# One Trainium2 core: a linear-attention, gated-unit and mixer kernel whose weight conversion, channel layer and one normalisation are rearranged

## The chip, the cores and the metric

The kernel runs on one core of a Trainium2 chip. Five engines work side by side: TensorE (PE in the profile; PEld is its weight load), VectorE (DVE), ScalarE (ACT), GpSimd (POOL) and SyncE (SP), which here only issues transfers; GpSimd issues some too. The metric is the device time of one execution in microseconds (us); lower is better.

## The reference

Three layers follow one another, on 4 batches of 768 tokens with 384 features (8 heads of 48). Weights are given as float64, all else as float32.

```python
# 1. delta-rule attention, a state of 48x48 per batch and head
k_n = k / (norm(k) + 1e-6)
for t in range(S):
    y[:, :, t] = einsum('bhd,bhde->bhe', q[:, :, t], state)
    v_old = einsum('bhde,bhd->bhe', state, k_n[:, :, t])
    state = state + beta_t * einsum('bhd,bhe->bhde', k_n[:, :, t], v[:, :, t] - v_old)
# 2. gated unit: x is [4, 768, 384]
h = gelu_tanh(x @ w_in)                      # 1024 columns
u, v = h[..., :512], h[..., 512:]
v_n = (v - mean(v)) / sqrt(var(v) + 1e-6) * g_ln
v_s = einsum('ts,bsd->btd', w_sg, v_n) + b_sg[None, :, None]
x = x + (u * v_s) @ w_out
# 3. token mixing, then channel mixing
u = x + (relu(x^T @ w_tok1) @ w_tok2)^T      # 768 -> 256 -> 768
out = u + relu(u @ w_ch1) @ w_ch2            # 384 -> 1536 -> 384
```

## The kernel before

The attention is computed in chunks of 64 tokens, in six groups g (two pairs of batches, three stretches of 256 tokens). For each group TensorE forms Gram products (`kk`, `qk`: L134 and L159), VectorE solves a triangular system in 31 steps (`solve`, L179 to L221: two operations a step, L209 and L211), its result td is copied by transfers into tw (L230, issued by SyncE), TensorE makes three small products of it (`merge`: L242, L252, L264), and then the `chain` of 16 steps runs through four chunks (L305, L291, L281). The chain needs yr, a product made on GpSimd by `vput` (L273). `vput(g+1,0)`, for the next group's first chunk, is issued in the last step of chain g, the later ones inside the chain. The order of the work is written out by hand: one string for every chain step in the table `ACT` at the end of the file names what is issued there: K and Q Gram products, m a part of a merge, S a step of the solve, v a `vput`, l the loads of v (by GpSimd), z zeroing, c a step of `beside`.

`beside` is `conv` (L491 to L494): the float64 words of w_in are turned into a float32 pair, high and low part. `load` does it in 12 pieces of 256 columns: a load on SyncE (L456), five VectorE operations (L469 to L476), a copy on ScalarE for the high part (L444), a subtraction on GpSimd (L445), and two GpSimd transfers into a scratch in DRAM (L487). The steps 'c' stand in chains 0 to 2, what is left runs ahead of chain 3. Tiles for it come from a pool of their own, which `room()` closes after that to make space for xn of batches 2 and 3. `zeros` (L108, L112) is 12 ScalarE copies of zeros into tiles of the attention: four before anything else, the rest one for each step of the first solve from step 9 on.

Every dense product is made of three matmuls (high x high, high x low, low x high), `mm3`, L547 to L549. With chain 5 the dense part begins (`start`, `pre`): the scratch is loaded into SA as w_in (L699), `trans(0)` transposes batch 0 (L571, evacuated in L564), `V(0)` makes the V half (six pieces of 512 columns) and `U(0)` the U half (eight pieces of 384). One step of these is issued for each step of chain 5. Two PSUM banks serve them until `rest` adds six. `evV` evacuates a piece of V: square (ScalarE, L577), L578 and L581 on VectorE around a Tanh (ScalarE, L580), mean and variance (L586, L587), a power on GpSimd (L589), the normalise on VectorE (L591), and the split into a high copy (ScalarE, L444) and a low part (GpSimd, L445). Beside this the conversions of w_sg and w_out run. Then `Sg`, `V`, `Out`, `U` and `trans` follow for the batches, then the token mixing.

The channel layer (`chan`, L657 to L677) takes 8 half-batches of 384 tokens. For each of 12 f it makes 9 matmuls, w_ch1 stationary and the tokens moving, a Relu on ScalarE (L638) and the low part on VectorE (L639); one f later 9 matmuls with those results stationary and w_ch2 moving add to three accumulators of 384 columns. At the end xn takes three adds (L676) and three transfers out (L677). The 18 transposes of a batch stand between the batches. The weights w_ch1 and w_ch2 are converted beside the token mixing and the first half-batch.

## Time and profile before

| | |
|---|---|
| time, median of 3 runs | 981.63 us (979.33 to 985.21) |
| the profiled execution's own time | 980.1 us |
| its span | 978.4 us |
| TensorE busy | 856.8 us (88%), 9644 instructions |
| VectorE busy | 613.8 us (63%) |
| ScalarE busy | 391.2 us (40%) |
| GpSimd busy | 338.2 us (35%) |
| chain that ended last | TensorE 65%, VectorE 19%, ScalarE 4%, issue 4%, transfers 3%, GpSimd 2% |

Busy times are sums over one execution. The chain that ended last is followed back from the last instruction, at each step to what released it. The stages: up to 95 us the first Gram products and the first solve; 95 to 267 the solves, merges and chains 0 to 3; 267 to 298 chain 4; 298 to 351 chain 5 with V and U of batch 0; 351 to 548 the gated unit; 548 to 657 its end and the token mixing; 657 to 978 the channel layer, its first half-batch up to 701.6.

### The profile page before, as it was taken

The page shows a single profiled execution, that of the slowest core. Times are in us where ns is not written, and L with a number is a line of the kernel's source. Part 1 is how long each engine was busy: PE and PEld are TensorE (multiplying, and loading weights), DVE is VectorE, ACT ScalarE, POOL GpSimd, SP SyncE. Part 2 cuts the span into 40 slices and gives each one's busy share as a digit, 9 for nine tenths or more (in the row PEclk, how much of TensorE's full clock was granted, in tenths as well). Part 3 has the DMA queues.
Part 4 walks back from the last instruction along what each step waited for, and adds up shares of the span by engine and source line. Part 5 has one row for each costly group of instructions (what it writes and reads, how often), then busy time and mean ns, then how long its engine had stood idle before and what let it go on. Part 6 is the DMA issues. An engine that isn't in the chain of part 4 may idle for free.

```text
span 978.4 us, 23130 instructions
## 1 busy us (share of the span) xinstructions
PE 856.8 (88%) x9644; PEld 812.9 (83%) x9644; DVE 613.8 (63%) x1254; ACT 391.2 (40%) x869; POOL 338.2 (35%) x434
## 2 busy tenths in 40 slices
PE   6456764878788899999999998989899999999998
PEld 4346764867787689999999987879899999999998
DVE  5999998989902787947839896878513213123122
ACT  4525543758787663423423432434212112112111
POOL 7330475777763534323234443834200000000000
PEclk9679776979999999999999997999999999999999
DMA  6564748675444040000000022224100000000000
GB/s 160 148 144 107 174 122 193 170 169 138 122 95 147 1 163 31 1 1 1 1 1 0 30 69 65 87 87 127 50 1 25 25 1 25 1 25 25 1 25 25
DMA packets 60344, 68.05 MB, mean 70 GB/s; under 512 B 30416, under 2 KB 37328, under 8 KB 60240
## 3 DMA queue, kind: packets, MB, share of 16 engines
q1 hardware_dynamic: 58288, 59.49, 23.3%
q0 software_dynamic: 1952, 7.08, 2.3%
q8 instruction: 76, 1.25, 0.5%
q14 instruction: 28, 0.23, 0.1%
HBM read 51.61 MB, written 7.86 MB: 61 GB/s over the span
## 4 chain that ended last, share of the span: by engine, by line
PE 65%; DVE 19%; ACT 4%; issue 4%; DMA 3%; POOL 2%; SPq 1%; DVEq 0%; ACTq 0%; POOLq 0%
PE ps L547 18%; PE ps L548 18%; PE ps L549 18%; DVE p L209 4%; DVE T L211 3%; DVE F L471 2%; DVE F L472 2%; DMA tw<-td 2%; PE yp L281 2%; PE gm L134 1%; PE gm L264 1%; PE ps L571 1%; DVE F L473 1%; PE ck L305 1%; PE gm L252 1%
## 5 line engine op out<-in xcount | busy, mean ns | idle before, releaser
L639 DVE SCALAR_TENSOR_TENSOR hlo<-ps,hh 128x384 fp32r<-128x384 f32 x96 | 53.5, 557 | 206.2 <-ACT hh L638 206.2
L638 ACT ACTIVATE hh<-ps 128x384 fp32r<-128x384 f32 x96 | 47.2, 491 | 227.1 <-PE ps L549 227.1
L547 PE MATMUL ps<-GU,SB 128*128 128x384 f32 x288 | 97.6, 339 | 0.0
L549 PE MATMUL ps<-GU,SB 128*128 128x384 f32 x288 | 97.5, 339 | 0.0
L548 PE MATMUL ps<-GU,SB 128*128 128x384 f32 x288 | 97.2, 338 | 0.0
L209 DVE TENSOR_TENSOR p<-Li,T 128x87 f32<-128x87 f32 (+15 forms) x186 | 81.2, 449 | 3.8
L211 DVE TENSOR_TENSOR T<-T,p 128x87 f32<-128x87 f32 (+15 forms) x186 | 74.2, 412 | 3.8
L548 PE MATMUL ps<-SB,VHt 128*128 128x384 f32 x192 | 65.0, 338 | 2.3 <-POOL SB L445 2.3
L549 PE MATMUL ps<-VHt,hlo 128*128 128x384 f32 x192 | 65.3, 340 | 1.3 <-DVE hlo L639 1.3
L547 PE MATMUL ps<-SB,VHt 128*128 128x384 f32 x192 | 65.0, 338 | 0.0
L547 PE MATMUL ps<-VHt,hh 128*128 128x384 f32 x192 | 65.0, 338 | 0.0
L548 PE MATMUL ps<-VHt,hh 128*128 128x384 f32 x192 | 64.6, 337 | 0.0
L549 PE MATMUL ps<-SB,VHt 128*128 128x384 f32 x192 | 64.5, 336 | 0.0
L614 POOL TENSOR_TENSOR q<-q,u 128x384 f32<-128x384 f32 x32 | 36.9, 1158 | 66.1 <-DVE q L613 66.1
L305 PE MATMUL ck<-yr,tw 128*64 128x48 f32 x768 | 38.1, 239 | 23.0 <-POOL yr L273 12.7
L273 POOL TENSOR_TENSOR yr<-v,nn 64x192 f32<-64x192 f32 x96 | 54.3, 566 | 9.0 <-DMA v<-in_vn_dram 2.2
L145 POOL TENSOR_SCALAR_AFFINE_SELECT aq<-aq 32x512 f32<-32x512 f32 x48 | 38.0, 791 | 55.6 <-ACT aq L142 50.7
L305 PEld LDWEIGHTS ck<-yr,tw 128*64 128x64 f32 x768 | 32.8, 151 | 26.8 <-POOL yr L273 14.7
L547 PE MATMUL ps<-X,SA 128*128 128x384 f32 x144 | 49.9, 346 | 5.8 <-DVE xn L626 3.2
L548 PEld LDWEIGHTS ps<-GU,SB 128*128 128x128 f32 x288 | 54.1, 188 | 0.9 <-DVE GU L564 0.9
L547 PEld LDWEIGHTS ps<-GU,SB 128*128 128x128 f32 x288 | 54.1, 188 | 0.6 <-DVE GU L564 0.6
L549 PEld LDWEIGHTS ps<-GU,SB 128*128 128x128 f32 x288 | 54.0, 188 | 0.3 <-POOL SB L445 0.3
(155 smaller groups left out, 2357.3 us busy)
## 6 DMA issues: line engine op xcount, KB each, us to landing
kq<-in_kq_dram SPq DMA_DIRECT2D x48, 256.0 KB, 4.3
st<-in_ch_dram SPq DMA_DIRECT2D x36, 256.0 KB, 2.8
...
```

The costliest lines, as they stand in the source:

```text
L145: if blk==0: nc.gpsimd.affine_select(out=a,in_=a,pattern=[[0,8],[-64,2],[1,32]],compare_op=ALU.is_gt,fill=0.0,base=0,channel_multiplier=-1)
L209: nc.vector.tensor_tensor(p,Li[:,j,j+1:].unsqueeze(1).to_broadcast([128,w,n]),T[:,:w,j].unsqueeze(2).to_broadcast([128,w,n]),ALU.mult)
L211: nc.vector.tensor_tensor(T[:,:w,j+1:],T[:,:w,j+1:],p,ALU.add)
L273: n0=8*h+cc; nc.gpsimd.tensor_tensor(YRs[bb][gc%3][T_[par],:,par,:],VS[bb][T_[par],n0:n0+7:2,:],NNs[g%3][T_[par],16*bb+n0:16*bb+n0+7:2].un ...
L281: nc.tensor.matmul(yps[bb][o0:o0+64,2*pair+par,:],aq[F_,par,pair,cc,:],yr[F_,pair,par,:],start=True,stop=True)
L305: nc.tensor.matmul(u2[T_[par],pair,:],tw[F_,par,16*bb+8*h+2*pair+cc,:],yr[F_,pair,par,:],start=True,stop=True)
L547: nc.tensor.matmul(ps,L[0],Rr[0],start=first,stop=False)
L548: nc.tensor.matmul(ps,L[0],Rr[1],start=False,stop=False)
L549: nc.tensor.matmul(ps,L[1],Rr[0],start=False,stop=last)
L614: nc.gpsimd.tensor_tensor(gt,gt,u2[:,d,t],ALU.mult)
L638: nc.scalar.activation(hi,ps,AF.Relu)
L639: nc.vector.scalar_tensor_tensor(lo,ps,0.0,R(hi),op0=ALU.max,op1=ALU.subtract)
```

## The change

- w_in: only the columns of the V half (six pieces) are converted through the scratch, in steps 8 to 15 of chain 4, two steps of the generator at a time, ahead of `vput(5,0)`. The tiles are parts of attention tiles that are no longer used (`Spare`). The high copy moves from ScalarE to VectorE. The U half (six pieces) is loaded and converted straight into SA beside `trans(0)` and `V(0)`, a piece step for every second of theirs, and what is left ahead of `U(0)`.
- zeros: none ahead of the first products; one for each step of the first solve from step 1 on.
- all four xn are allocated at the start; `room` goes, and an unused branch on `qd`.
- V: the normalise is an Identity activation on ScalarE with scale rs and bias sf = -mean x rs, which a VectorE operation on one column makes.
- channel layer: six blocks of 512 tokens. The transposes of the next block (`tblk`) are issued within the present one from f = 6 on, into one of two buffers UB. In the second product w_ch2 is stationary and the 512 tokens move, so the output is transposed (OT); `out` adds the high and the low part of the block's input in two VectorE operations of 512 columns, and one transfer for each third of the features follows. The host's `unpack` turns the output back.

The diff, cut to what is spoken of:

```diff
-        for _ in range(4): next(zs)
@@ phase_a, first solve
-            if ns>8: next(zs,0)
+            if ns>0: next(zs,0)
@@ phase_a
+        class Spare:
+            def __init__(self):
+                v=lambda t,o,n:t.rearrange("p a b -> p (a b)")[:,o:o+n]
+                self.b=dict(st=[v(Lis[0],0,512),v(Lis[0],512,512),v(MD,0,512)],F=[v(MD,512,256),v(MD,768,256)],
+                    sq=[PP[0][:,0:256]],sh=[v(Ts[0],0,256),v(Ts[0],256,256)],sl=[v(Ts[0],512,256),v(Ts[0],768,256)])
...
-            if g==3 and beside is not None:
-                for _ in beside: pass
-                room()
+            if g==4 and beside is not None: bs=beside(Spare())
             if g==5 and tail is not None:
                 while wait: tick()
+                for _ in bs: pass
...
-                    if a=='c' and beside is not None: next(beside,0)
+                    if a=='c':
+                        for _ in range(n_): next(bs,0)
@@ load
-                    split(Fs[j],w[0],w[1],True)
+                    nc.vector.tensor_copy(w[0],Fs[j]); nc.gpsimd.tensor_tensor(w[1],Fs[j],R(w[0]),ALU.subtract)
@@ conv
-        yield from load(I['win'],None,None,[(0,3072,0)],pool=PX,lag=cfg.get('lag',1),g=cfg.get('cg',2),out=...)
+        yield from load(I['win'],None,None,[(1024*k+512,1024*k+1024,512*k) for k in range(3)],pool=PX,out=...)
@@ late2
-            L.UT=[a.rearrange("p (k t) -> p k t",t=768) for a in hl(GU,0,2304)]
+            L.UB=[[a.rearrange("p (k t) -> p k t",t=512) for a in hl(GU,3072*i,1536)] for i in range(2)]
@@ evV
+            sf=PT.tile([128,1],F32,name="sf")
             yield 1
-            nc.vector.tensor_scalar(v2,v2,mv[:,0:1],rs,ALU.subtract,ALU.mult)
+            nc.vector.scalar_tensor_tensor(sf,mv[:,0:1],-1.0,rs,op0=ALU.mult,op1=ALU.mult)
             yield 1
+            nc.scalar.activation(v2,v2,AF.Identity,bias=sf,scale=rs)
             split(v2,VH[0][:,s],VH[1][:,s],True)
@@ channel layer
+        def tblk(i):
+            for k in range(3):
+                ps=bank()
+                for j in range(4):
+                    b,n=divmod(4*i+j,6)
+                    nc.tensor.transpose(ps[:,128*j:128*j+128],xn[b][:,n,128*k:128*k+128],idt)
+                push(evT(ps,L.UB[i%2][0][:,k],L.UB[i%2][1][:,k]))
+                yield 1
-        def chan(b,hf,need):
-            acc=[psB[2].tile([128,512],F32,name="ps")[:,:384] for _ in range(3)]
+        def chan(i,need,nxt):
+            acc=[psB[2].tile([128,512],F32,name="ps") for _ in range(3)]
+            ut=L.UB[i%2]; hd=[None]*12
+            def out(e):
+                o=ph[0].tile([128,512],F32,name="o",bufs=2)
+                nc.vector.tensor_tensor(o,acc[e],R(ut[0][:,e]),ALU.add)
+                nc.vector.tensor_tensor(o,o,R(ut[1][:,e]),ALU.add)
+                nc.sync.dma_start(OT[:,e,512*i:512*i+512],o)
...
-                    for i in range(3):
-                        mm3(acc[i],[h[:,128*i:128*i+128] for h in hd[f-1]],[w[:,f-1,:] for w in C2A] if f<9 else [w[:,f-9,:] for w in L.C2B],f==1,f==12)
+                    for e in range(3):
+                        w=[w[:,f-1,128*e:128*e+128] for w in C2A] if f<9 else [w[:,f-9,128*e:128*e+128] for w in L.C2B]
+                        mm3(acc[e],w,hd[f-1],f==1,f==12)
+                        if f==12: out(e)
                     yield 1
+                if f>5: next(nxt,0)
@@ pre
-            for h in (1,0):
-                for i in range(2):
-                    nc.sync.dma_start(R(WIN[i])[:,:,512*h:512*h+512],scr[i].rearrange("p (k f) -> p k f",f=1024)[:,:,512*h:512*h+512])
-            yield from trans(0,XT)
-            yield from V(0)
+            for i in range(2): nc.sync.dma_start(R(WIN[i])[:,:,512:1024],scr[i].rearrange("p (k f) -> p k f",f=512))
+            ld=lw('win',WIN,[(1024*k,1024*k+512,1024*k) for k in range(3)])
+            yield from both(trans(0,XT),ld,cfg['u0'])
+            yield from both(V(0),ld,cfg['u1'])
+            for _ in ld: pass
             yield from U(0)
@@ rest
-                for b in range(4):
-                    go(both(chan(b,0,need),ld,n[2])); go(both(chan(b,1,need),ld))
-                    if b<3: go(trans(b+1,L.UT))
+                for i in range(6):
+                    go(both(chan(i,need,tblk(i+1) if i<5 else iter(())),ld,n[2]))
@@ tables
+for i in range(8,16): ACT[4][i]+=' c2'
```

## Rows read from the trace of the kernel before

**Rows 1.** stages: stretch, length, busy us (instructions) by engine, PE clock, DMA share, GB/s

```profile
95.00:267.00 172.00, 123.94 (x3586) 116.50 (x3587) 161.75 (x354) 102.97 (x244) 116.57 (x183) 0.83 0.65 156
267.00:298.00 31.00, 26.76 (x923) 25.20 (x923) 1.82 (x1) 25.62 (x61) 16.77 (x32) 1.00 0.41 89
298.00:351.00 53.00, 47.00 (x527) 39.26 (x523) 32.10 (x58) 35.33 (x81) 21.69 (x30) 0.97 0.36 127
351.00:548.00 197.00, 194.67 (x1081) 186.70 (x1080) 146.49 (x270) 79.09 (x166) 69.11 (x71) 1.00 0.03 9
...
657.00:701.60 44.60, 39.57 (x217) 37.68 (x217) 35.54 (x90) 18.48 (x51) 17.27 (x19) 1.00 0.27 83
701.60:978.40 276.80, 273.01 (x1568) 271.21 (x1566) 67.48 (x125) 48.52 (x102) 0.00 (x0) 1.00 0.05 18
```

**Rows 2.** waits from 95 to 299 us: us in total, times, longest

```profile
PE gm L242 <- DMA tw<-td: 17.9, 7, 7.1
...
DVE Li L183 <- DMA md<-gf: 2.2, 1, 2.2
```

**Rows 3.** SyncE's queue in time: start us, us; idle before in brackets

```profile
156.62 4.95 SPq L230 DMA_DIRECT2D tw<-td  x4
```

**Rows 4.** TensorE in time: chain 1's start, a merge, chain 5's start

```profile
128.82 1.68 PE L305 MATMUL ck<-yr,tw 128*64 128x48 f32 x18 [4.92 <-POOL yr L273]
...
162.40 0.29 PE L242 MATMUL gm<-tw,G 128*32 128x32 f32 x2 [7.14 <-DMA tw<-td]
166.65 1.07 PE L242 MATMUL gm<-tw,G 128*32 128x32 f32 x32 [3.96 <-DMA tw<-td]
...
298.26 1.11 PE L305 MATMUL ck<-yr,tw 128*64 128x48 f32 x31
```

**Rows 5.** VectorE by line, 95 to 267 us: busy us, mean ns; conversion, first and last

```profile
L469 DVE TENSOR_TENSOR sq<-st 128x256 f32<-128x256 f32 x12 | 6.3, 568 | 0.0
...
L471 DVE TENSOR_SCALAR F<-st 128x256 int32<-128x256 int32 x12 | 4.9, 447 | 0.0
```

**Rows 6.** GpSimd in time before chain 1

```profile
126.32 0.75 POOL L445 TENSOR_TENSOR sl<-F,sh 128x256 fp32r<-128x256 f32 x1
...
128.14 1.79 POOL L273 TENSOR_TENSOR yr<-v,nn 64x192 f32<-64x192 f32 x3
```

**Rows 7.** ScalarE in time at the start: zeros

```profile
7.01 3.99 ACT L108 COPY aq<-XZ 64x1024 f32<-64x1024 f32 x4 [4.94 <-DVE XZ L92]
```

**Rows 8.** GpSimd in time before chain 5

```profile
289.09 1.11 POOL L79 DMA_DIRECT2D v<-in_vn_dram  x2
...
292.42 2.25 POOL L273 TENSOR_TENSOR yr<-v,nn 64x192 f32<-64x192 f32 x4 [2.22 <-DMA v<-in_vn_dram]
```

**Rows 9.** VectorE in time, normalise of V(0) pieces

```profile
317.02 0.55 DVE L591 TENSOR_SCALAR q<-q,mv,rs 128x512 f32<-128x512 f32 x1 [0.16 <-POOL rs L589]
...
328.12 1.52 DVE L591 TENSOR_SCALAR q<-q,mv,rs 128x512 f32<-128x512 f32 x1
```

**Rows 10.** ScalarE by line, 400 to 548 us, shapes apart: high copy of V

```profile
L444 ACT CAST VHt<-q 128x512 fp32r<-128x512 f32 x15 | 9.3, 617 | 26.4 <-DVE q L591 26.4
```

**Rows 11.** waits from 298 to 351 us

```profile
PE ps L547 <- DVE q L581: 4.7, 5, 2.1
```

**Rows 12.** TensorE in time: V(0) pieces begin; 512-column matmuls

```profile
308.44 0.50 PE L547 MATMUL ps<-SA,X 128*128 128x512 f32 x1
...
311.67 0.50 PE L547 MATMUL ps<-SA,X 128*128 128x512 f32 x1
...
380.08 0.39 PE L547 MATMUL ps<-SA,X 128*128 128x512 f32 x1
...
382.12 0.39 PE L547 MATMUL ps<-SA,X 128*128 128x512 f32 x1
```

**Rows 13.** stage of one channel half-batch

```profile
701.65:739.60 37.95, 37.95 (x218) 37.92 (x218) 8.29 (x16) 5.91 (x12) 0.00 (x0) 1.00 0.05 16
```

**Rows 14.** VectorE in time at the end

```profile
973.60 1.60 DVE L676 TENSOR_TENSOR xn<-xn,ps 128x384 f32<-128x384 f32 x3 [1.00 <-PE ps L549]
```

More of the change, by code (lines that the diff above doesn't have):

```diff
@@ L28, in pack, with phase_a @@
     return dict(kq=half(tr(K)),qt=half(tr(Q)),vn=natv(V),kn=kn,bt=c(bt).reshape(2,3,128,32))
-def phase_a(tc,I,xn,cfg,tail=None,beside=None,room=None):
+def phase_a(tc,I,xn,cfg,tail=None,beside=None):
     nc=cfg.get('wrap',lambda x:x)(tc.nc)
@@ L389, in phase_a, with tile @@
         vput(0,0)
+        class Spare:
[3 more added lines that the diff above has]
+                    sq=[PP[0][:,0:256]],sh=[v(Ts[0],0,256),v(Ts[0],256,256)],sl=[v(Ts[0],512,256),v(Ts[0],768,256)])
+                self.n={}
+            def tile(self,shape,dt,name,bufs=1):
+                b=self.b[name]; assert len(b)>=bufs,(name,bufs)
+                i=self.n[name]=self.n.get(name,-1)+1
+                x=b[i%bufs].bitcast(dt) if dt!=F32 else b[i%bufs]
+                return x.rearrange("p (a b) -> p a b",b=2) if len(shape)==3 else x
         kt=[12]; mt=[8]
@@ L491, in load, with conv @@
             yield 1
-    def conv(PX,scr):
-        yield from load(I['win'],None,None,[(0,3072,0)],pool=PX,lag=cfg.get('lag',1),g=cfg.get('cg',2),out=lambda r:(scr[0][:,r],scr[1][:,r]))
+    def conv(scr,PX):
+        yield from load(I['win'],None,None,[(1024*k+512,1024*k+1024,512*k) for k in range(3)],pool=PX,out=lambda r:(scr[0][:,r],scr[1][:,r]))
     me.conv=conv
@@ L795 @@
 _m=dict(m=(0,1,9,10,11,12,13,14)); _k=dict(K=(1,2,5,6))
[L796 to L797 removed]
+ACT=[_row([3]*6+_st[6:],K=(3,4,6,7),Q=(9,10,12,13),m=range(9,15),l=(9,),v=(15,),q=(14,)),
+     _row(_st,z=(0,),**_k,**_m,**_s),_row(_st,z=(0,),**_k,**_m,**_s),_row(_st,z=(0,),**_m,**_s),
      _row([3]*9+[0]*7,z=(0,),m=(0,1,8,9,10,11,12,13,14,15),Q=(4,5,6,7),l=(9,),v=(15,)),_row([0]*16)]
[L799 removed]
+for i in range(8,16): ACT[4][i]+=' c2'
+CFG={'nl':(0.5,0.2,0.7),'k0':(1,3,5,7),'q0':(11,13,15,17),'l1':20,'late':2,'far':3,'tl':2,'half':21,'hs':5,'u0':0.5,'u1':0.5,'act':ACT}
 def build(tc,I,O,cfg):
     with tc.tile_pool(name="per",bufs=1,side="right") as pp, tc.tile_pool(name="scr",bufs=1,space=bass.MemoryType.DRAM) as pd, tc.manual_schedule():
[L803 removed]
+        xn=[pp.tile([128,6,384],F32,name=f"xn{b}") for b in range(4)]
         d=_dense(tc,I,O,xn,cfg)
[L805 to L814 removed]
+        scr=[pd.tile([128,1536],F32,name=f"scr{i}") for i in range(2)]
+        phase_a(tc,I,xn,cfg,lambda:d.start(scr),lambda P:d.conv(scr,P))
+        d.rest()
 def kernel(**inputs):
```

34 lines of the change are left out of this document (7 added, 27 removed).

## The prediction

> **What bounds the kernel now.** I read the table by stages first, since the shares of the whole span mix stages with different limits [rows 1]. It falls into three parts. From 351 us to the end TensorE is the bound: 194.67 us busy of 197, and 273.01 of 276.8 at a granted clock of 1.00. There only fewer or shorter matmuls help, or fewer stalls at the seams: the first channel half-batch takes 44.6 us, the next 37.95. Before 267 us nothing is full: between 95 and 267 TensorE is busy 123.94 us of 172, at a granted clock of 0.83, and VectorE 161.75. A busy share of 94% suggests that VectorE sets the pace, and the change takes work from it. The waits of that stretch say less [rows 2]: TensorE waits 17.9 us for the transfer of the solved matrices (tw<-td), and VectorE itself stands 2.2 us for its own input (md<-gf). The queues show what stands between: SyncE issues the four tw loads only from 156.62, after the loads ahead of it, and takes 4.95 us for them [rows 3], and TensorE's waits for that one set are 7.14 and 3.96 us, 11.1 of the 17.9 [rows 4]. So at least there VectorE was not last.
>
> From 298 to 351 (last chain, V and U of batch 0) TensorE is busy 47.0 of 53 us with VectorE and ScalarE at 32.1 and 35.3 [rows 1].
>
> **The change part by part.**
>
> *The conversion leaves chains 0 to 2.* Twelve pieces go, each five VectorE operations, from 568 to 447 ns on the average, five lines of 12, together 28.6 us [rows 5], a copy on ScalarE, a subtraction of 0.75 us and two DMA issues on GpSimd, and a load on SyncE. What of this is on the path?
> - GpSimd: at chain 1's start TensorE waits 4.92 us for yr [rows 4]. The products on GpSimd that make it began at 128.14, right behind a subtraction of the conversion that began at 126.32 [rows 6]; another such piece stands ahead of that, so two pieces, 1.82 us each (126.32 to 128.14), 3.64 us, are removed from just this wait. I take -3.6, bounds 0 (ScalarE's part is late next) and -4.9 (the wait vanishes).
> - VectorE: 28.6 us come off an engine that is 94% busy. TensorE can get back at most what it waits for the solves: 17.9 us. Of these the 11.1 us above are SyncE's and the DMA's. That leaves 6.8. VectorE, once faster, stands longer for md<-gf, whose chain through TensorE, ScalarE and SyncE is not shortened. I take -4, nearest to the 6.8; bounds 0 and -17.9.
> - SyncE: twelve loads less ahead of md and tw; -1, bounds 0 and -3 (an estimate: a load's issue is taken as a tw issue, 4.95/4 = 1.2 us, and two or three of them stand ahead of a late load).
> Together -8.6.
>
> *Zeros.* Four ScalarE copies of 1 us stand at 7.01 to 11.0, ahead of the first copies of Gram products [rows 7]. They are spread over the first solve, a step at a time, which ScalarE has time for. But TensorE's first products end only shortly before and the solve starts later through a DMA; -1.5, bounds -4.0 (all four) and +1 (a zero now stands ahead of a copy of a later group).
>
> *The V half in chain 4.* VectorE is idle there (1.82 us busy of 31 [rows 1]), so its 6 times 5 operations, and the copy that moves to it, cost nothing. The cover is that idle stretch, which ends with the last chain's transposes; without it they would cost about 17 us (half of 28.6 and six copies at about half a microsecond). GpSimd has no such room. Its queue runs v loads at 289.09 and then the products for chain 5 at 292.42, ready at 294.67 [rows 8]; TensorE starts chain 5 at 298.26 [rows 4]. The change puts six subtractions and twelve DMA issues ahead of those products: 6 x (0.75 + 2 x 0.555) = 11.2 us, behind the v loads' end at 290.2. The products then run 301.4 to 303.6, and chain 5 starts 5.3 us later. Behind the same queue stand the identity for the transposes, the two small scalings and the next products, so nothing of it comes back at once. Before, GpSimd waited for DMAs there, which will have landed; I take +5.0, bounds +2 (the subtractions start earlier than 290.2, as GpSimd's masks of the last group come earlier) and +7 (the loads of w_in from scratch late too).
>
> *U half beside trans(0) and V(0), normalise on ScalarE.* Per piece of V VectorE gives up the normalise, which took 0.55 us alone and 1.52 us beside a GpSimd subtraction [rows 9], and gets a tiny operation. It gets six pieces of four operations in place. ScalarE gets an Identity pass over 512 columns, priced like its 512-column copy at 617 ns [rows 10]. So per piece: VectorE has four passes of 512 columns, 3 x 0.55 + 1.52 = 3.2 us at the least, and comes to 1.7 plus about 2 us of conversion; ScalarE goes from three passes to four, 1.85 to 2.47 us, plus the chain's copies and a conversion's, an estimated 3.7, against 3.2 us that pass on TensorE for a piece (308.44 to 311.67 [rows 12]). TensorE's wait on VectorE here is 4.7 us in all [rows 11]. I take 0: the gain on one engine is the loss on the other; bounds -3 (most of the 4.7 goes) and +6 (ScalarE is late by 0.5 to 1 us a piece, for six pieces, which was VectorE's place).
> The Trainium skill, "ScalarE: Activation LUTs", section "Rules for kernel authors", says to leave adds and multiplies to VectorE. In the rows the pass on ScalarE (about 0.62 us) and on VectorE (0.55 us) alone are about equal, and beside GpSimd VectorE's is 2.5 times that; by the page the move costs 0.07 us a piece, 1.7 us over 24 pieces if all of it were on the path, by the rows nothing.
>
> *V of batches 1 to 3.* TensorE takes 9 matmuls of 226.7 ns, 2.04 us, for a piece (first and tenth start 380.08 and 382.12 [rows 12]); VectorE took the 3.2 us a piece, and yet TensorE was full [rows 1], as the eight PSUM banks cover a V of six pieces and Sg or Out follow. ScalarE's 2.47 us a piece falls behind by 0.4 x 6 = 2.5 us, less than VectorE did. 0; bounds -1 and +2.
>
> *Channel layer.* Before: 8 halves of 216 matmuls of 384 columns, 37.95 us each when nothing stalls [rows 13], 175.7 ns a matmul, with what small gaps there are. 384 columns at 2.4 GHz are 160, so 15.7 ns belong to the instruction and not to its columns. The 512-column step of 226.7 has nearly the same: 213.3 + 13.4. After: 6 blocks of 216 at 213.3 + 15.7 = 229, 49.5 us, 296.8 in all against 303.6: -6.8 (bounds 0, the extra in proportion to columns, and -9.8, at 226.7). The first block has the weights' conversion beside it, which cost 44.6 - 37.95 = 6.7 us; each f now gives a third more time, so I take 3 of it to go, -3 (0 to -6.7). Transposes are 72 either way, but sit within a block: a wait at the seams is hidden rather than made, -0.5. At the end, before: three adds of 384 in 1.60 us, at 973.60, then the DMA [rows 14]. After: each third of the output gets two adds of 512, about 0.7 us each by their size, but the first two thirds are done while TensorE runs the last f's remaining matmuls only if the order lets them; the last third alone adds 1.4 us, and its neighbour some: +0.5 to +2.5, taken at +1.5. Sum -8.8, with the output of the whole layer in fewer DMAs -9; bounds +2 and -16.
>
> **Sum.** -8.6 - 1.5 + 5.0 + 0 + 0 - 9 = -14.1. The profiled execution took 980.1 us (span 978.4 and 1.7 around it), so 966.0; the median of the three runs lies 1.5 above it, at 981.63, so a median of about 967 is to be expected.
>
> **The rivals.**
> - *VectorE is the bound of chains 0 to 3 after all.* For: 161.75 of 172 us busy. Against: TensorE's waits for tw are SyncE's for 11.1 of 17.9 us. Then -17.9 instead of -4: 953, with warmer clock some less.
> - *ScalarE and GpSimd crowd the last chain.* For: 3.7 us of ScalarE's work a piece against 3.2 of TensorE's, and GpSimd has subtractions of V, of U's conversion and of w_sg together with the chain's products. Against: ScalarE was busy only 35.3 of 53 us. Price: +6 at V(0) and +3 as the last two pieces of the U half are forced ahead of U(0): 976.
> - *The matmul's cost goes by its columns.* Were the extra in the 384-column step spread over its columns, 512 would cost 234 ns and turning the product round would save nothing of the 6.8: 974. Against it speaks the 226.7 of V's rows; for it, that these have other operands. By the Trainium skill, "TensorE: Matmul & The Clock Gate", section "Wait — 56ns, not 53.3ns?", the fixed part is about 2.5 ns a matmul; 432 matmuls fewer would then be worth 1.1 us by it. The rows show 13 to 16 ns.
> - *Slower: ScalarE's queue is held.* The Identity pass stands in ScalarE's order behind nothing but its scalars, which come from GpSimd's power, and that can stand behind the subtraction of the piece before, which is what slows the normalise to 1.52 us [rows 9]. The squares and Tanhs of the next pieces, which free the PSUM banks, queue behind the waiting pass. Before, VectorE waited in that place. It decides once a piece takes over 3.2 us on average in V(1) to V(3), so that six pieces overrun by more than the banks hold: at 4.5 us a piece against 2.04, 14.8 us a V, of which the banks cover about 7, three times, +23: 990. Against: in V(1) to V(3) VectorE's 3.2 us a piece cost TensorE nothing that is seen.
>
> **How the numbers follow.** Forecast 0.52 (961 to 972), VectorE the bound 0.13, crowding 0.16, columns 0.1, held queue 0.09. The range takes in forecast, crowding, columns and the nearer part of the VectorE case: 951 to 978. A measurement can tell about 0.5%, 4.9 us: faster is below 976.7. Faster: 0.52 + 0.13 + 0.1 and half of the crowding, 0.83; same 0.08, slower 0.09.
>
> **What would show it.** Right: no wait of about 5 us at chain 1's start; VectorE's waits for md longer; products for chain 5 on GpSimd ready later against the end of its v loads by 11 us; steps of 227 ns in the channel layer; 217 matmuls in about 49.5 us. Wrong: chain 5's start earlier by over 15 us, TensorE below 190 of 197 us busy in the stage of V(1) to V(3), a first channel block that stalls over 5 us, or steps of 234 ns.

## The result, and the profile after

The changed kernel takes 989.95 us (median of 20 runs, 983.94 to 997.16) against 983.43 for the kernel before (20 runs, 975.91 to 988.99). The ratio is 1.0071, with a 95% interval of 1.0047 to 1.0095: slower by about 7 us, where 967 were forecast. The profiled execution spans 988.1 us, the one before 978.4. Ratios leave out executions that took over 1.5% longer than the fastest of the same kernel, as four of e1's twelve, two of e8's and the profiled one of e12 did, of which no row is used.

Where each stage begins is read from the first matmul of the stage in the profiled execution of each kernel (us from the span's start). Single executions of the same attention differ by up to 6 us at chain 4 (255.6 to 262.0 in the changed kernel, e2, e3, e4 and e15), so only the larger differences count.

| kernel | chain 0 | chain 4 | chain 5 | V(0) | U(0) | Sg(0) | V(1) | last matmul | span |
|---|---|---|---|---|---|---|---|---|---|
| before | 78.1 | 265.3 | 298.2 | 308.4 | 330.3 | 351.3 | 380.1 | 974.3 | 978.4 |
| changed | 77.5 | 255.6 | 295.9 | 310.9 | 336.5 | 362.4 | 392.8 | 980.8 | 988.1 |
| GpSimd free (e1) | 79.2 | 258.0 | 290.7 | 310.0 | 335.0 | 360.2 | 389.0 | 974.8 | 981.8 |
| kept busy (e2) | 80.0 | 261.1 | 302.3 | 317.4 | 342.5 | 368.3 | 398.6 | 986.3 | 993.6 |
| no U conversion (e3) | 80.7 | 256.9 | 298.3 | 312.3 | 333.5 | 353.8 | 384.9 | 973.0 | 980.0 |
| normalise on VectorE (e4) | 80.5 | 259.2 | 299.4 | 314.0 | 341.0 | 364.2 | 393.0 | 979.2 | 986.5 |
| channel layer alone (e5) | 77.0 | 264.2 | 294.1 | 306.6 | 328.5 | 351.3 | 381.5 | 970.8 | 977.9 |
| conversion early (e7) | 80.6 | 258.5 | 294.0 | 307.6 | 332.6 | 358.4 | 388.7 | 976.0 | 983.1 |
| both halves by scratch (e8) | 80.9 | 255.1 | 290.6 | 316.4 | 337.6 | 357.8 | 388.8 | 976.0 | 983.2 |
| the same, loads ahead (e9) | 78.2 | 256.5 | 295.9 | 311.3 | 332.5 | 352.7 | 381.5 | 967.3 | 975.7 |
| and third buffer (e10) | 80.0 | 259.9 | 296.1 | 317.2 | 338.4 | 358.7 | 388.7 | 975.7 | 981.9 |
| and zeros as before (e11) | 78.2 | 261.1 | 297.0 | 316.8 | 338.0 | 358.2 | 387.0 | 972.9 | 979.2 |
| channel layer and end (e13) | 77.5 | 268.4 | 300.9 | 311.0 | 332.9 | 355.7 | 385.9 | 973.1 | 979.3 |
| old conversion, no GpSimd (e14) | 78.9 | 272.7 | 304.6 | 315.0 | 336.9 | 357.8 | 387.7 | 982.1 | 986.2 |
| U half sooner (e15) | 78.7 | 262.0 | 304.8 | 324.6 | 347.7 | 367.9 | 397.8 | 984.4 | 991.7 |

The two first lines tell the story. At chain 4 the changed kernel is 9.7 us ahead. Chain 4 then takes 40.3 us in place of 32.9, chain 5 to V(0) 15.0 in place of 10.2, V(0) and U(0) 51.5 in place of 42.9: at Sg(0) it is 11.1 us behind. From its first product of the channel layer to the last matmul it gains 5.4 us, and after that matmul it loses 3.2.

The loss begins in the GpSimd queue between chains 4 and 5 (changed kernel, GpSimd in time; L495 and L496 are the subtraction and the transfers of the V half, L270 the products; to compare with [rows 8]):

```profile
279.69 1.11 POOL L79 DMA_DIRECT2D v<-in_vn_dram  x2
280.87 0.72 POOL L495 TENSOR_TENSOR T<-md,T 128x256 fp32r<-128x256 f32 x1
...
293.57 0.72 POOL L495 TENSOR_TENSOR T<-md,T 128x256 fp32r<-128x256 f32 x1 [0.90 <-DVE T L495]
294.23 1.10 POOL L496 DMA_DIRECT2D scr<-T  x2
295.35 2.27 POOL L270 TENSOR_TENSOR yr<-v,nn 64x192 f32<-64x192 f32 x4
...
300.49 0.23 POOL L523 TENSOR_SCALAR gh<-gh 128x4 f32<-128x4 f32 x1 [2.20 <-DMA gh<-in_g_dram]
...
303.43 4.76 POOL L270 TENSOR_TENSOR yr<-v,nn 64x192 f32<-64x192 f32 x8
```

TensorE in the same stretch, against [rows 4]: its last matmuls of chain 4, then the wait.

```profile
288.56 1.08 PE L261 MATMUL gm<-tw,kn 128*48 128x64 f32 x31
295.92 2.84 PE L302 MATMUL ck<-yr,tw 128*64 128x48 f32 x32 [6.29 <-POOL yr L270]
```

Of the first 32 matmuls of chain 5, 31 took 1.11 us before [rows 4]; the 32 take 2.84 here. TensorE starts when the first of GpSimd's four products for them is made, and the last is ready only at 297.62. The clock has fallen as well (stages: stretch, length, busy us of PE, PEld, DVE, ACT, POOL, granted clock, DMA share, GB/s):

```profile
255.60:289.00 33.40, 27.94 (x952) 26.24 (x952) 14.90 (x27) 26.37 (x62) 23.39 (x41) 1.00 0.58 153
289.00:296.00 7.00, 0.71 (x24) 0.57 (x19) 4.21 (x11) 1.87 (x4) 5.08 (x10) 0.87 0.28 99
296.00:304.00 8.00, 7.80 (x84) 6.18 (x85) 1.44 (x3) 3.33 (x10) 4.84 (x9) 0.50 0.62 202
304.00:312.00 8.00, 8.00 (x84) 6.46 (x83) 4.72 (x10) 4.89 (x14) 4.46 (x8) 0.50 0.56 194
312.00:316.00 4.00, 4.00 (x41) 2.98 (x40) 1.49 (x4) 0.93 (x3) 0.00 (x0) 0.67 0.22 68
316.00:320.00 4.00, 3.89 (x44) 3.03 (x45) 1.66 (x3) 3.95 (x9) 0.00 (x0) 1.00 0.00 0
```

After the stand, TensorE runs at a granted clock of 0.50, that is 1.2 GHz, up to 312 us and beyond, in stretches in which it is busy 7.80 and 8.00 of 8 us.

U(0) begins with two gaps (TensorE in time), which were not there before:

```profile
337.43 0.34 PE L559 MATMUL ps<-X,SA 128*128 128x384 f32 x1
340.68 0.44 PE L557 MATMUL ps<-X,SA 128*128 128x384 f32 x1 [2.91 <-ACT SA L453]
...
345.36 0.69 PE L557 MATMUL ps<-X,SA 128*128 128x384 f32 x1 [3.43 <-DVE q L591]
```

And the waits from 296 to 363 us, to compare with [rows 11]:

```profile
PE ps L557 <- DVE q L591: 8.0, 5, 3.4
...
PE ps L557 <- ACT SA L453: 2.9, 1, 2.9
```

The normalise, by line (393 to 560 us; busy us, mean ns, idle before): the pass on ScalarE, and the operation on one column that VectorE got for it.

```profile
L605 ACT ACTIVATE q<-q,sf,rs 128x512 f32<-128x512 f32 x18 | 14.6, 812 | 15.4 <-DVE sf L603 15.4
```
```profile
L603 DVE SCALAR_TENSOR_TENSOR sf<-mv,rs 128x1 f32<-128x1 f32 x18 | 19.0, 1058 | 2.8 <-POOL rs L599 1.6
```

The channel layer, a block between its fourth and fifth transposes (stage), two of its matmuls fifteen steps apart, and VectorE at the end, to compare with [rows 13] and [rows 14]:

```profile
804.20:855.50 51.30, 51.30 (x230) 41.62 (x229) 14.34 (x21) 8.94 (x15) 0.00 (x0) 1.00 0.04 16
```
```profile
977.31 0.40 PE L559 MATMUL ps<-hh,SW 128*128 128x512 f32 x1
...
980.81 0.39 PE L559 MATMUL ps<-hh,SW 128*128 128x512 f32 x1
```
```profile
983.39 0.69 DVE L685 TENSOR_TENSOR o<-ps,GU 128x512 f32<-128x512 f32 x1 [0.80 <-DMA out_dram<-o]
984.12 0.69 DVE L686 TENSOR_TENSOR o<-o,GU 128x512 f32<-128x512 f32 x1
```

A block takes 51.30 us with 216 products and 12 transposes; with the 0.11 us of a transpose that leaves 50.0, 231 ns a product (233 in the last rows). The last two of six adds stand 0.80 us for the transfer of the first output tile, since two buffers serve three tiles.

### The profile page after: what moved, and what is told of

Its sections match the earlier page's. It is cut to its first block, busy times and chain, and to the rows that moved or that the text cites. A ratio compares the mean times of both kernels' runs of the same rounds, so it can differ in the third digit from the quotient of the medians.

```text
span 988.1 us, 22192 instructions
## 1 busy us (share of the span) xinstructions
PE 853.0 (86%) x9211; PEld 753.0 (76%) x9212; DVE 612.5 (62%) x1236; ACT 407.7 (41%) x863; POOL 330.2 (33%) x422
## 3 DMA queue, kind: packets, MB, share of 16 engines
HBM read 50.04 MB, written 6.29 MB: 57 GB/s over the span
## 4 chain that ended last, share of the span: by engine, by line
PE 61%; DVE 15%; POOL 6%; DMA 5%; issue 5%; ACT 5%; SPq 2%; DVEq 0%; POOLq 0%; ACTq 0%
PE ps L558 18%; PE ps L557 18%; PE ps L559 18%; DMA tw<-td 3%; DVE F L480 2%; POOL yr L270 2%; DVE F L481 2%; DVE p L206 2%; DVE T L208 1%; POOL aq L142 1%; DVE F L482 1%; PE yp L278 1%; PE gm L239 1%; PE gm L249 1%; POOL aq L143 1%
## 5 line engine op out<-in xcount | busy, mean ns | idle before, releaser
L652 DVE SCALAR_TENSOR_TENSOR hlo<-ps,hh 128x512 fp32r<-128x512 f32 x72 | 49.7, 690 | 168.7 <-ACT hh L651 168.7
L651 ACT ACTIVATE hh<-ps 128x512 fp32r<-128x512 f32 x72 | 43.1, 598 | 214.5 <-PE ps L559 214.5
L557 PE MATMUL ps<-GU,SB 128*128 128x512 f32 x216 | 86.7, 402 | 1.9 <-DVE xn L639 1.9
L558 PE MATMUL ps<-GU,SB 128*128 128x512 f32 x216 | 85.6, 396 | 0.2 <-DVE GU L574 0.2
L559 PE MATMUL ps<-GU,SB 128*128 128x512 f32 x216 | 85.4, 395 | 0.2 <-POOL SB L454 0.2
L206 DVE TENSOR_TENSOR p<-Li,T 128x87 f32<-128x87 f32 (+15 forms) x186 | 76.8, 425 | 4.1
L558 PE MATMUL ps<-SB,VHt 128*128 128x384 f32 x192 | 65.6, 341 | 2.3 <-POOL SB L454 2.3
L557 PE MATMUL ps<-SB,VHt 128*128 128x384 f32 x192 | 65.7, 342 | 0.0
L559 PE MATMUL ps<-SB,VHt 128*128 128x384 f32 x192 | 65.2, 340 | 0.0
L557 PE MATMUL ps<-X,SA 128*128 128x384 f32 x144 | 50.7, 352 | 9.7 <-DVE q L591 3.6
L270 POOL TENSOR_TENSOR yr<-v,nn 64x192 f32<-64x192 f32 x96 | 54.7, 569 | 7.0
L558 PE MATMUL ps<-hlo,VHt 128*128 128x512 f32 x144 | 56.5, 393 | 0.3 <-DVE hlo L652 0.3
L557 PE MATMUL ps<-hh,VHt 128*128 128x512 f32 x144 | 56.6, 393 | 0.0
L559 PE MATMUL ps<-hh,VHt 128*128 128x512 f32 x144 | 56.6, 393 | 0.0
L559 PE MATMUL ps<-X,SA 128*128 128x384 f32 x144 | 50.0, 347 | 0.2 <-POOL SA L454 0.2
L239 PE MATMUL gm<-tw,G 128*32 128x32 f32 x768 | 19.9, 215 | 34.9 <-DMA tw<-td 32.3
L558 PE MATMUL ps<-X,SA 128*128 128x384 f32 x144 | 49.9, 346 | 0.0
```

What stands on the lines that cost most here:

```text
L206: nc.vector.tensor_tensor(p,Li[:,j,j+1:].unsqueeze(1).to_broadcast([128,w,n]),T[:,:w,j].unsqueeze(2).to_broadcast([128,w,n]),ALU.mult)
L239: nc.tensor.matmul(xp[r1,u,:],G21[F_,16*bb+u,:],tw[F_,par,16*bb+u,0:32],start=True,stop=True)
L270: n0=8*h+cc; nc.gpsimd.tensor_tensor(YRs[bb][gc%3][T_[par],:,par,:],VS[bb][T_[par],n0:n0+7:2,:],NNs[g%3][T_[par],16*bb+n0:16*bb+n0+7:2].un ...
L557: nc.tensor.matmul(ps,L[0],Rr[0],start=first,stop=False)
L558: nc.tensor.matmul(ps,L[0],Rr[1],start=False,stop=False)
L559: nc.tensor.matmul(ps,L[1],Rr[0],start=False,stop=last)
```

## The experiments

Ratios are to the kernel before, run on the same chip with each; the changed kernel's is 1.0071.

**e1, GpSimd free.**

```diff
-nc.vector.tensor_copy(w[0],Fs[j]); nc.gpsimd.tensor_tensor(w[1],Fs[j],R(w[0]),ALU.subtract)
-for x,y in zip(out(r),w): nc.gpsimd.dma_start(x,R(y))
+nc.vector.tensor_copy(w[0],Fs[j]); nc.vector.tensor_tensor(w[1],Fs[j],R(w[0]),ALU.subtract)
+for x,y in zip(out(r),w): nc.sync.dma_start(x,R(y))
```

> The changed kernel with the V half's six subtractions on VectorE and its twelve scratch transfers issued by SyncE, so that GpSimd's queue is free ahead of chain 5's first products. In the changed kernel TensorE stood from 288.6 to 295.92 us there and ran at a granted clock of 0.50 from 296 to about 314 us. Theory (queue and clock): the stand of 7.3 us goes, and with it the slow clock, which cost 4.8 us between chain 5's start and V(0) and 1.6 us in V(0)'s first piece: about 13 us less than the changed kernel, near 976.5. Rival 1 (the queue alone, the clock's loss is hidden by the chain's waits): 7 us less, near 983. Rival 2 (the crowding of V(0) and U(0) is the limit and takes up what comes early): U(0) ends no earlier against the span's start than in the changed kernel, near 989.

985.99 us, 1.0007 (0.9971 to 1.0043): better than the changed kernel by 4 us by the medians and 6 by the ratios, not by 13. The stand before chain 5 is gone (32.7 us from chain 4 to 5), but V(0) starts 19.4 us after chain 5, not 10.2. The stand has moved to the first transposes (TensorE, then GpSimd, in time):

```profile
297.74 0.90 PE L581 MATMUL ps<-idt,xn 128*128 128x128 f32 x3 [5.82 <-POOL idt L520]
```
```profile
297.06 0.10 POOL L518 MEMSET mh<- 128x1 f32 x1 [6.42 <-DMA scr<-T]
```

GpSimd waits 6.42 us for a scratch transfer before it may write mh, ahead of the identity: these tiles of the dense part lie where the conversion's borrowed tiles lay, and the last transfer still reads them. So the gate is the end of the conversion and of its transfers, wherever TensorE shows the wait. Rival 1 comes nearest in size, but not for its reason: the stand did not go, it moved.

**e2, TensorE kept busy.**

```diff
+ACT[4][15]+=' W30'
```

> The changed kernel with 30 idle matmuls of 512 columns (on a tile of zeros, results unused) issued to TensorE between chain 4 and chain 5, that fill most of the 7.3 us in which it stood. The stand itself remains, since GpSimd's queue is as it was. Theory (clock): the granted clock stays at 1.00 from 296 to 314 us, chain 5's start to V(0) falls from 15.0 to about 10.2 us and V(0)'s first piece by 1.6: 5 to 6.5 us less than the changed kernel, near 984. Rival (the clock's loss is hidden): within 1.5 us of the changed kernel, near 990, whatever the clock.

995.16 us, 1.0115 (1.0073 to 1.0157): no gain. The clock did what was wanted (TensorE in time, then stages as above):

```profile
295.04 6.42 PE L331 MATMUL wm<-dum 128*128 128x512 bf16 x29 [0.16 <-issue]
302.30 0.32 PE L302 MATMUL ck<-yr,tw 128*64 128x48 f32 x2 [0.84 <-POOL yr L270]
...
310.18 0.32 PE L302 MATMUL ck<-yr,tw 128*64 128x48 f32 x2 [1.10 <-POOL yr L270]
```
```profile
302.00:310.00 8.00, 5.88 (x92) 4.59 (x92) 2.05 (x4) 4.32 (x12) 5.03 (x10) 1.00 0.63 202
310.00:314.00 4.00, 2.35 (x35) 1.77 (x35) 0.47 (x2) 0.29 (x1) 3.47 (x8) 0.91 0.86 325
314.00:318.00 4.00, 3.60 (x37) 2.90 (x38) 3.19 (x7) 3.46 (x11) 0.79 (x2) 0.50 0.24 69
```

At full clock up to 310 us, chain 5 to V(0) still takes 15.1 us. The first 32 matmuls take 2.41 us even so (302.30 to 304.71), as GpSimd is still making yr. For the products of chain 5's next chunk, which stand behind the scalings on GpSimd, TensorE waits 1.10 us where it was slow before. And ScalarE stands for the load of the U half's first piece, ahead of the copies that chain 5 needs (ScalarE in time):

```profile
313.71 0.43 ACT L477 ACTIVATE sq<-st 128x256 f32<-128x256 f32 x1 [4.12 <-DMA st<-in_win_dram]
```

The clock's loss in the changed kernel lay beside these waits; a cost of its own is not to be seen, but the run doesn't rule one out, since the clock is at 0.50 again from 314 us on, in V(0)'s first piece. That the median lies 5 us above the changed kernel's is not explained: in the profile chain 4 already starts 5.5 us later, ahead of the edit, and the two intervals overlap.

**e3, no U conversion.**

```diff
-for i in range(2): nc.sync.dma_start(R(WIN[i])[:,:,512:1024],scr[i].rearrange(...))
-ld=lw('win',WIN,...); yield from both(trans(0,XT),ld,cfg['u0']); yield from both(V(0),ld,cfg['u1'])
-for _ in ld: pass
+for h in (1,0):
+    for i in range(2): nc.sync.dma_start(R(WIN[i])[:,:,512*h:512*h+512],scr[i].rearrange(...))
+yield from trans(0,XT)
+yield from V(0)
```

> The changed kernel without the conversion of w_in's U half: both halves of SA are filled from the scratch of the V half, so U is computed from the V half's columns. All of the U half's loads, VectorE and ScalarE operations and GpSimd subtractions beside trans(0) and V(0) are left out. The late queue before chain 5 stays. Theory: this conversion is what holds V(0) and U(0): TensorE's two gaps at U(0)'s start, 337.6 to 340.7 and 341.8 to 345.4 us, go (6.7 us), and some of the 8.0 us of waits of V(0) on VectorE: 7 to 10 us less, near 981.5. Rival (the normalise on ScalarE is what holds them): under 3 us less, near 988.

979.34 us, 0.9949 (0.9915 to 0.9984): 10.6 us less than the changed kernel by the medians and 12 by the ratios, as the theory said and a little more. V(0) and U(0) take 41.5 us (51.5 in the changed kernel). The late queue is still there: chain 4 takes 41.4.

**e4, normalise on VectorE.**

```diff
-nc.vector.scalar_tensor_tensor(sf,mv[:,0:1],-1.0,rs,op0=ALU.mult,op1=ALU.mult)
-nc.scalar.activation(v2,v2,AF.Identity,bias=sf,scale=rs)
+nc.vector.tensor_scalar(v2,v2,mv[:,0:1],rs,ALU.subtract,ALU.mult)
```

> The changed kernel with V's normalise back on VectorE, as before. Theory (the normalise is about neutral: VectorE's one-column operation takes 1.06 us on the average beside GpSimd, nearly what the whole normalise took, and ScalarE's pass takes 0.81): within 2 us of the changed kernel, near 990. Rival (ScalarE's extra pass is what makes V(0) and U(0) late): 5 us less, near 985. Other rival (the pass on ScalarE is a gain): 3 us more, near 993.

988.67 us, 1.0086 (1.0055 to 1.0117): the same as the changed kernel. The normalise's place is neutral within these intervals, some 3 us.

**e5, the channel layer alone**, on the kernel before: `tblk`, the new `chan`, `UB`, `OT` and `unpack` of the diff, nothing else.

> The kernel before with the channel layer of the change alone (six blocks of 512 tokens, second product turned round, transposed output). From the two traces: the layer's matmuls take 6.4 us less from its first transpose to the last matmul, since a 512-column step in it takes 231 ns and not the 229 of the forecast, and the end after the last matmul takes 7.3 us in place of 4.1: 3.2 us less in all, a ratio near 0.997. The forecast's own step says 9 us less, 0.991. Rival (the layer is no gain, the attention's part made the difference in the traces): 1.000.

979.58 us, 0.9971 (0.9945 to 0.9997): 3 us, as the traces said, a third of the forecast.

**e7, conversion early**, on e1.

```diff
+ACT[4][0]='c1 '+ACT[4][0]
```

> The changed kernel with the V half's subtractions on VectorE and its transfers by SyncE (as in the run with GpSimd free), and with the first two loads of w_in issued in step 0 of chain 4 rather than step 8, ahead of the tw loads, so that VectorE can begin when the last solve ends (about 256 us) and not 14 us later. Theory (what holds the dense part is the end of the conversion: identity, small loads and tiles wait for its last transfer, wherever TensorE shows the wait): the conversion ends about 10 us earlier, TensorE stands for none of it, V(0) starts about 10 us after chain 5 and that one 33 us after chain 4: 8 to 12 us less than the run with GpSimd free alone, near 976. Rival 1 (the loads of the later pieces, behind the tw loads, set the end): 3 us less, near 983. Rival 2 (U half beside V(0) takes it back): 985.

981.73 us, 0.9983 (0.9946 to 1.0020), 4 us less than e1 by the medians and 2.4 by the ratios, whose intervals overlap: nearest to rival 1. The conversion ends at 290 us, the identity no longer waits for it (GpSimd in time), and V(0) comes 13.6 us after chain 5. What remains is ScalarE, which stands with the Square of the U half's first piece (ScalarE in time):

```profile
293.50 0.10 POOL L518 MEMSET mh<- 128x1 f32 x1 [3.18 <-ACT yr L290]
```
```profile
303.91 0.44 ACT L477 ACTIVATE sq<-st 128x256 f32<-128x256 f32 x1 [3.53 <-DMA st<-in_win_dram]
```

The releaser of mh is a copy of chain 4, not a transfer of the conversion. But the Square waits 3.53 us for the U half's load, and the copies that chain 5 needs stand behind it, the next at 304.25.

**e8 and e9, both halves through the scratch** in chain 4, on e7; `pre` loads both halves from it, as in e3. e9 has more buffers for it and issues four loads ahead. The main lines:

```diff
 e8
-[(1024*k+512,1024*k+1024,512*k) for k in range(3)]
+[(1024*k+512*(1-h),1024*k+512*(1-h)+512,1536*h+512*k) for h in range(2) for k in range(3)]
-for i in range(8,16): ACT[4][i]+=' c2'
+for i in range(8,16): ACT[4][i]+=' c3'
 e9, besides
-self.b=dict(st=[v(Lis[0],0,512),v(Lis[0],512,512),v(MD,0,512)],...
+g=[v(G21s[k],256*m,256) for k in range(2) for m in range(4)]
+self.b=dict(st=[v(Lis[0],0,512),v(Lis[0],512,512),v(MD,0,512),v(Ts[0],0,512),v(Ts[0],512,512)],...,sh=g[0:4],sl=g[4:8])
```

> As the run with the early conversion, but all twelve pieces of w_in go through the scratch in chain 4, the V half first, and nothing is converted beside trans(0) and V(0). Theory: V(0) and U(0) take 42 us as before, 8 to 10 less than in the changed kernel; the conversion, 12 pieces at some 2.7 us from 256 us, ends near 290 to 295, as in the run with GpSimd free alone, so V(0) starts near 308. Sum near 976 to 978. Rival (twelve pieces end after 300 us; the identity waits for them): V(0) at 316 or later, 984 or more.

> As the run with both halves through the scratch, but with five buffers for the loads and four for the two parts (more attention tiles that are no longer used), so that four loads of w_in are issued in step 0 of chain 4, ahead of the tw loads, and VectorE need not wait for SyncE to send the first parts. Theory (the end of the conversion, when it is later than the end of chain 4, sets V(0); nothing beside V(0) then costs anything): twelve pieces at 2.7 us from 258 us end near 291, not 302; V(0) starts near 306, U(0) and the rest as in the run with both halves through the scratch: 8 to 11 us less than that one, near 974. Rival (twelve pieces still end behind 300 us since the transfers of parts and loads share SyncE's queue with the tw loads): 980 or more.

e8: 983.07 us, 0.9986 (0.9957 to 1.0015). e9: 982.57 us, 1.0002 (0.9970 to 1.0034). V(0) and U(0) take 41.5 us in both, which confirms e3 with nothing left out. But V(0) comes 25.8 and 15.3 us after chain 5: the rivals. In e9 the last part is made at 298.2 us, and the release tells the rest (GpSimd in time):

```profile
300.39 0.10 POOL L519 MEMSET mh<- 128x1 f32 x1 [10.64 <-DMA scr<-G]
```

Whatever is converted last in borrowed tiles holds the dense part.

**e10 and e11, the end and the zeros**, on e9 and e10.

```diff
 e10
-o=ph[0].tile([128,512],F32,name="o",bufs=2)
+o=ph[0].tile([128,512],F32,name="o",bufs=2) if i<5 else R(ph[0].tile([128,512],F32R,name="hh"))
 e11, besides
+for _ in range(4): next(zs)
 ...
-if ns>0: next(zs,0)
+if ns>8: next(zs,0)
```

> As the run before it in this list, and in the last channel block the output tiles rotate over the three buffers of hh in place of two of their own. In the changed kernel the last two adds waited 0.80 us for the transfer of the first output tile, after a matmul end at 981.2 us. Theory: 0.8 to 1.5 us less after the last matmul, 6.5 us or less in place of 7.3; the medians of the two differ by about that, which they can hardly show, so the trace is to tell.

> As the run before it in this list, with the zeros as in the kernel before: four copies ahead of the first Gram copies, the rest from step 9 of the first solve on. In the traces the first solve begins near 15 us with the change's order and at 19.2 with the old one, but chain 0 begins at 77.5 to 80.9 us in six profiles with the change's order and at 78.1 and 77.0 with the old one, with a granted clock of 0.59 to 0.76 just before it. Theory (what the first solve gains is lost to the slower clock before chain 0): chain 0 begins near 77.5, within 3 us of the other order, and the time is the same within 2 us. Rival (the prediction's step: the old order costs): 1.5 to 4 us more.

e10: 982.63 us, 0.9992 (0.9963 to 1.0022). From the last matmul to the end it takes 6.2 us, 1.1 less than the changed kernel; the time can't show that. e11: 981.40 us, 0.9988 (0.9958 to 1.0017), with chain 0 at 78.2 us. The old place of the zeros costs nothing that can be seen.

**e12 and e13, for a faster kernel.** e13 is e5 with e10's end. e12 adds to e13 a split of the conversion: the U half in chains 1 and 2 as before, the V half in chain 4 as in e7.

```diff
 e12
+def vhalf(PX,scr): ...  # columns of V, subtraction on VectorE, transfers by SyncE
-c=(4,10,12,14) in chain 0; c=(1,4,7,9,12,15) in chain 1; c=(1,4,7,9,12,14) in chain 2
+c=(1,4,7,9,12) in chain 1; c=(1,4,7,9) in chain 2
+ACT[4][0]='d1 '+ACT[4][0]
+for i in range(8,16): ACT[4][i]+=' d2'
```

> The kernel before with the new channel layer (last block's output tiles in the buffers of hh), and with w_in split as follows: the U half (six pieces) converted as before in chains 1 and 2, with GpSimd, none of it in the step that makes chain 1's or chain 3's first products; the V half in chain 4 as in the run with the early conversion. Nothing is converted beside V(0). Zeros and normalise as before. Theory: chain 4 starts about 4 us before the old 264 to 265 us (half of the 7 that the whole conversion's absence gives), the handover to the dense part is like the old one (V(0) 10 to 12 us after chain 5), V(0) and U(0) take 42 to 43 us, and the channel layer gives 3 + 1.3 us: 6 to 8 us less than the kernel before, ratio near 0.993. Rival (the V half in chain 4 holds the handover even so): chain 4 to chain 5 or chain 5 to V(0) longer by 3 us or more, ratio 0.997, no better than the channel layer alone.

> The kernel before with the new channel layer alone, and in its last block the output tiles rotate over the three buffers of hh. Theory: the 3 us of the channel layer and 1.3 us of the end: ratio near 0.9955. Rival (the end's wait is only moved to the transfer): 0.997, as the channel layer alone.

e12: 976.02 us, 0.9905 (0.9872 to 0.9938), faster than both kernels. Why it gains is not shown beyond the expectation. e13: 980.69 us, 0.9935 (0.9897 to 0.9973); the theory's 0.9955 and the rival's 0.997 both lie in that interval, and e12's overlaps it, so what the split adds to the channel layer is not clear of noise.

**e14, the old conversion without GpSimd**, on the kernel before.

```diff
-split(Fs[j],w[0],w[1],True)
-for x,y in zip(out(r),w): nc.gpsimd.dma_start(x,R(y))
+split(Fs[j],w[0],w[1],False)
+for x,y in zip(out(r),w): nc.sync.dma_start(x,R(y))
```

> The kernel before with its conversion in chains 0 to 2, but the twelve subtractions on VectorE (about 5 us more for it) and the twenty-four transfers issued by SyncE: GpSimd has nothing of the conversion. Theory of the forecast (of the gain of the chains 3.6 us are GpSimd's queue at chain 1, and VectorE is not last): chain 1 starts 3 to 4 us earlier against chain 0 than in the kernel before (50.8 us) and the time falls by 3 us, ratio 0.997. Rival (VectorE's load sets the pace): chains 2 to 4 later by about 5 us, ratio 1.005.

990.85 us, 1.0053 (1.0030 to 1.0077). Both are half right. Chain 1 starts 45.2 us after chain 0 (50.8 before), and TensorE's wait there is 0.66 us, not 4.92. But chain 4 starts at 272.7. That is not VectorE's load (waits of VectorE from 95 to 272 us, and its stage):

```profile
DVE sl L445 <- ACT sh L444: 23.8, 4, 10.0
```
```profile
95.00:267.00 172.00, 114.68 (x3408) 107.18 (x3408) 144.26 (x359) 96.68 (x231) 85.06 (x134) 0.83 0.61 150
```

VectorE is busy 144.26 us here, less than before [rows 1]: the subtraction, now in its order, waits for ScalarE's copy, and the solves stand behind it. SyncE's twenty-four added transfers may delay chain 4 too; the run doesn't separate them. It bears out GpSimd's term and leaves VectorE's open.

**e15, the U half sooner.**

```diff
-'u0':0.5,'u1':0.5
+'u0':1.0,'u1':1.0
```

> The changed kernel with a step of the U half's conversion for every step of trans(0) and V(0), not every second one, so that it is done within V(0)'s first pieces and nothing is left ahead of U(0). Theory (part of its cost is what is forced between V(0) and U(0), 6.7 us of gaps there, while VectorE and ScalarE are a third busy during trans(0)): the gaps at U(0)'s start go, 4 to 6 us less than the changed kernel, near 985. Rival (the conversion's operations, in order on ScalarE behind their loads, hold the last chain as much as they held U(0)): V(0) starts 3 us or more later after chain 5 than the 15.0 us of the changed kernel, and the time stays within 2 us, near 990.

992.53 us, 1.0062 (1.0031 to 1.0093): the rival. U(0) has no gaps (20.2 us to Sg(0), 26.0 in the changed kernel), but V(0) comes 19.8 us after chain 5. ScalarE in time:

```profile
316.20 0.44 ACT L477 ACTIVATE sq<-st 128x256 f32<-128x256 f32 x1 [5.58 <-DMA st<-in_win_dram]
```

It stood 5.58 us for the load, ahead of the last evacuations of the transposes. What is saved at U(0) is lost at V(0).

## Why the prediction was wrong

Term by term, as the runs have it: chains 0 to 3 with the zeros -7.7 us for -10.1, the V half some +13 from chain 4 to V(0) for +5, the U half +8.6 for 0, the channel layer -3.0 for -9. That makes about +11 for -14.1; the span grew by 9.7 and the time by 7.

*Chains 0 to 3 and the zeros, forecast -10.1.* Not far off in sum. The attention with the new schedule starts chain 4 at 255.1 to 262.0 us in ten profiles (changed, e1 to e4, e7 to e10, e15), 258.3 on the average; with the old one at 265.3, 264.2 and 268.4, 266.0: -7.7. GpSimd's term was there, and was put too low: TensorE's wait at chain 1's start falls from 4.92 us [rows 4] to 1.26, the 3.6 of the forecast, but chain 0 to chain 1 takes 44.7 us on the average of the ten and 52.3 of the three, 7.5 less. e14, with VectorE still loaded, has 45.2, so this is mostly GpSimd's (changed kernel, TensorE in time):

```profile
121.27 0.32 PE L302 MATMUL ck<-yr,tw 128*64 128x48 f32 x2 [1.26 <-POOL yr L270]
```

From chain 1 to chain 4 only 2.3 us are gained, where VectorE and SyncE were put at 5. Most of VectorE's freed time became waiting, though not for md alone. Before, from 95 to 267 us, it waited 2.2 us for md [rows 2] and for ScalarE:

```profile
DVE rc L192 <- ACT sh L188: 3.9, 2, 2.9
```

In the changed kernel, from 95 to 255 us:

```profile
DVE Li L180 <- DMA md<-gf: 13.2, 2, 11.9
DVE rc L189 <- ACT sh L185: 9.5, 2, 5.1
DVE Li L180 <- DMA kq<-in_kq_dram: 4.3, 1, 4.3
```

Those are 27.0 us, 20.9 more than before, against the 28.6 taken off it [rows 5]. So the rival that VectorE is the bound, worth 17.9, falls, though how the rest of the gain divides between VectorE and SyncE is not settled. The zeros' -1.5 is not to be seen: the first solve starts at 14.67 us, not 19.24, but chain 0 does not start earlier (79.6 on the average of the ten, 77.9 in before, e5, e11, e13 and e14), and e11 gives the same time.

*V half in chain 4, forecast +5 (+2 to +7).* The queue was right, and so was where the products would be late: they began 14.6 us behind the end of the v loads (280.80 to 295.35) where 11.2 were reckoned, and the difference is GpSimd's waits for VectorE's parts, 3.5 us. Chain 4 takes 41.18 us on the average in the five profiles with this queue (changed, e2 to e4, e15) and 31.74 in the three of the old schedule: +9.4, over the upper bound. Not seen at all was what follows: that tiles of the dense part wait for the conversion's last transfer. In the changed kernel SyncE waits for it with the load of gh (SyncE's waits, 284 to 312 us):

```profile
SPq L521 <- DMA scr<-T: 12.8, 1, 12.8
```

So that load is issued at 297.33 us, 1.4 behind chain 5's start; before it was 0.5 ahead of it (297.69). GpSimd waits 2.20 us for it, and its next products begin 7.5 us behind chain 5's start, not 5.3 (before: 303.49). Chain 5 to V(0) takes some 4 us more too (14.7 on the average of changed, e2, e3 and e4, against 10.2, 12.6 and 10.2). How these divide between this queue, ScalarE's stand for the U half's load (e2) and the clock is not settled: from 296 to 311 us of the changed kernel TensorE is at 0.50 without a gap and hides the waits. The step that failed is "Behind the same queue stand the identity for the transposes, the two small scalings and the next products", priced inside the 5. The cover that was named, VectorE's idle stretch, did hide VectorE's time; nobody asked when its work would begin and end. Its last part came at 293.5 us: SyncE issued the loads of w_in only from 266.20, behind the tw loads (258.67, 7.49 us long), and VectorE began 14.61 us into its idle stretch:

```profile
270.66 0.58 DVE L478 TENSOR_TENSOR p<-Li 128x256 f32<-128x256 f32 x1 [14.61 <-DMA Li<-in_win_dram]
```

*U half beside V(0), forecast 0 (-3 to +6).* This is the largest miss beside the V half's. It cost 8.6 us in the trace, and leaving it out saves 10.6 us (e3). The step that failed is "the gain on one engine is the loss on the other". The normalise's leaving made little room on VectorE: in V(0) it took 1.21 us on the average (L591, six pieces), and the operation on one column 0.56 (L603), 3.9 us less in all, while the four operations for each of six pieces of the U half (L480 to L485) took 13.3. Nor is it a matter of busy time, which is what the forecast added up: VectorE is busy 36.3 and ScalarE 34.6 of the 51.5 us. TensorE's waits rose from 4.7 us [rows 11] to 11.1, 8.0 of them for VectorE and 2.9 for the U half's high copy on ScalarE; two of these, 2.91 and 3.43 us, are the gaps at U(0). The other 2.3 us are its matmuls, busy 40.3 us and not 38.0, at granted clocks of 0.93 and 0.87 in V(0) and U(0) against 1.00 and 0.92. The rival "crowding" had the mechanism and a price of +9 (+6 at V(0) and +3 at U(0), where 3.7 and 5.0 came), but was put at 0.16; it was set beside the forecast and not into it, though the forecast's own sum had ScalarE at 3.7 us a piece against 3.2.

*Channel layer, forecast -9.* -3.0 by e5. Its larger terms: a product takes 231 ns, not 229, which leaves 303.6 - 6 x 50.0 = 3.6 of the 6.8; the first block takes 56.4 us against 51.3 for the others, so 1.6 of the stall's 6.7 go and not 3; the end takes 7.3 us and not 4.1, +3.2 for +1.5, since six adds follow one another there; with a third buffer it takes 6.2 (e10).

*V(1) to V(3) and the held queue.* No effect, as forecast: TensorE is busy 167.00 of 167 us from 393 to 560. The 990 us of the held-queue rival are what was measured, by chance: its mechanism did not come. By the Trainium skill, "ScalarE: Activation LUTs", section "Rules for kernel authors", the normalise belonged on VectorE, at 1.7 us by the forecast's rows; e4 finds no difference.

*The rival of costs by columns* was nearer than it was given credit for: 231 to 233 ns stand between 227 and 234. The forecast took the 13 to 16 ns beyond the columns, read from two products, for a property of the instruction. The 2.5 ns that the Trainium skill states in "TensorE: Matmul & The Clock Gate", section "Wait — 56ns, not 53.3ns?", are not what these rows show: 231 less 213.3 for the columns leaves 18.

Of the prediction's signs of being wrong only one came, narrowly, the first block's stall (5.1 us for 5). None of them would have told of a late V(0) or U(0), where the time went.
